# Wider last output-projection products and four unused products around the second layer norm in a one-core decode block

## The chip, the core and the metric

The kernel runs on one core of one Trainium2 chip. The metric is the device time of one execution in microseconds, the median of several runs. A profile of one execution comes with it: when each instruction ran on TensorE (matmuls, PE, and their weight loads, PEld), VectorE (DVE), ScalarE (ACT), GpSimd (POOL) and SyncE (SP), what each waited for, when DMA transfers landed, and which share of its full clock TensorE was granted.

## What is computed

One decode step of a transformer block for four sequences with one token each. The model width is 512. The vector `c` gives six modulation vectors per sequence. The block is attention over the last 1024 cached positions (32 query heads over 8 key/value heads of 128), then a feed-forward layer with 1792 hidden units and ReLU; both have a layer norm in front and a gate behind.

```python
mod = (silu(c) @ w_mod).reshape(4, 6, 1, 512)
sa, ca, ga, sb, cb, gb = (mod[:, i] for i in range(6))
h = layernorm(x) * (1 + ca) + sa
x = x + ga * attention(h, k_cache, v_cache, wq, wo)   # ... @ wo at its end
h = layernorm(x) * (1 + cb) + sb
x = x + gb * (relu(h @ w1) @ w2)
```

Weights and caches are bfloat16; about 32 MB are read from HBM in one execution.

## The kernel before

Every engine's order is the order in which the program is written (a manual schedule). All large loads are issued by SP in one order: `w_mod`, two tiles of the key cache, `wq`, the other keys, the value tiles, `wo` in four parts, `w1`, and `w2` in five chunks that get smaller (512, 512, 384, 256 and 128 KB; they hold the hidden blocks 0 to 3, 4 to 7, 8 to 10, 11 to 12, and 13). Tiles are recycled, so a load is issued when its buffer is free; `w1` and `w2` lie in one buffer, `w12`, that `w_mod` used first.

TensorE's stages: transpose `c` and `x`; transpose keys; modulation products; the first layer norm's sums (a matmul with a matrix of 1/512); query products; scores, key tile by key tile; after the softmax, transposes of the probabilities and products with the values (`oT_ps`, L360); a reordering (`o4_ps`, L410). Then comes the region of the change:

- L424: the first half of the products with `wo`. The attention output, padded to 32 columns per part, is the stationary operand and 512 columns of `wo` stream, in four column groups, into `y4_ps`. DVE and ACT copy the result to `y4` in f32 (L428, L429).
- L432: four f32 products that fold `y4` into the transposed result `y_ps`, with `sel_b` (4 columns) as the moving operand. The profile shows each f32 product as two passes.
- L436: the second half of the products with `wo`. Now blocks of `wo` are stationary, taken with a step of four columns, and the 4 real columns of `o4` stream; 64 products, accumulated into `y_ps`. The first 32 need the third part of `wo`, the others the fourth.
- L441 to L445 on DVE: the gate, the residual sum (`s2`, and `xs2` for later) and its square. L447: one product with the 1/512 matrix gives mean and mean square for the second layer norm (`s_ps`).
- L194 from L451: `closing` turns `xs2` into the layout of the output (`x12_ps`, shown as x_ps). `closing` issues pairs of products with 32 columns of weights each in two column groups.
- L453 to L464 on DVE and ACT: mean, centred value times gain (`ab`), variance, and its inverse root (`rstd2`).
- L484, in `ffn1`: the products with `w1`, 32 for the first eight hidden blocks and 24 for the other six. The moving operand has 8 real columns, repeated four times (32). DVE scales by `rstd2`, adds and applies ReLU (L487 to L490) into `uT32`.
- L194 from L500 and L506: the products with `w2`, again through `closing`, four per hidden block, into `za_ps` (blocks 0 to 3 and 6 to 8) and `z_ps` (the others). 128 columns of `w2` stream in each.
- L502 to L511: ACT copies `za_ps`, DVE multiplies by the gate and adds `x12_ps` (`zc`); when `z_ps` is done, DVE makes `zg` (L509) and `res` (L511), and two DMAs write the output.

`sc_ps`, the PSUM tile of the scores (two banks of 512 columns), is last read by the softmax.

Of the kernel before, what the change touches and what calls it, by code (L numbers as in the profile page):

```python
# [9 lines left out]
ALU = mybir.AluOpType  # L10
AX = mybir.AxisListType
bf16 = mybir.dt.bfloat16
f32 = mybir.dt.float32
# [4 lines left out]
def kernel(  # L18
# [14 lines left out]
    nc = tc.nc  # L33
    P = 128
    B, Sq, D = A_x.shape
# [5 lines left out]
    DT = D // P  # L41
# [3 lines left out]
    CG = 32  # L45
# [17 lines left out]
    const = ctx.enter_context(tc.tile_pool(name="const", bufs=1))  # L63
# [4 lines left out]
    psA = ctx.enter_context(tc.tile_pool(name="psA", bufs=6, space=bass.MemoryType.PSUM))  # L68
# [34 lines left out]
    for h in range(Hkv):  # L103
        vt_ = kvpool.tile([P, NI, Dh], bf16, tag="kv", name=f"v{h}")
        nc.sync.dma_start(
            out=vt_[:].rearrange("p j d -> p (j d)"),
            in_=A_v_cache[:, h, S - W:, :].rearrange("b (p j) d -> p b (j d)", j=NI),
# [5 lines left out]
    NP = Hkv // 2  # L113
    wo_sb = wts.tile([P, NP, NL, D], bf16, tag="big", name="wo_sb")
# [13 lines left out]
    for (m0, e) in W2_CHUNKS:  # L128
        nc.sync.dma_start(out=w2_dst[:, m0 * D:(m0 + e) * D],
                          in_=B_w2[m0 * P:(m0 + e) * P, :].rearrange("(q e) n -> q (e n)", e=e))  # L130
# [3 lines left out]
    ident_bf = const.tile([P, P], bf16, name="ident_bf")  # L134
# [10 lines left out]
    ident_f = const.tile([P, P], f32, name="ident_f")  # L145
# [6 lines left out]
                          in_=ident_f[:].rearrange("p (k c) -> p k c", k=4)[:, :, 0:NX * B:NX])  # L152
# [2 lines left out]
    eps_t = const.tile([P, 1], f32, name="eps_t")  # L155
    nc.gpsimd.memset(eps_t[:], EPS)

    sel_b = const.tile([P, B], f32, name="sel_b")
    nc.vector.tensor_reduce(out=sel_b[:], in_=ident_f[:].rearrange("p (l c) -> p c l", c=CG)[:, 0:B, :], axis=AX.X, op=ALU.add)

    sel_o = const.tile([P, NL, 2, P // NL], bf16, name="sel_o")
    nc.gpsimd.memset(sel_o[:], 0.0)
# [5 lines left out]
    o4 = const.tile([P, NL, 2, 2, CG], bf16, name="o4")  # L168
# [17 lines left out]
    def rows(tile3, j, x):  # L186
        return tile3[:, j, NX - x:NX - x + CG]

    def closing(parts):
        for x in range(NX):  # L190
            for (ps, q, j, src, rhs, start, stop, cols) in parts:
                for g in range(2):
                    q0 = (q + g) * CG
                    nc.tensor.matmul(out=ps[q0:q0 + CG, cols], lhsT=rows(src, j, x), rhs=rhs(2 * x + g),  # L194
                                     start=start and x == 0, stop=stop and x == NX - 1, tile_position=(0, q0))
# [21 lines left out]
    sc_ps = psS.tile([P, W], f32, tag="s", name="sc_ps")  # L217
# [15 lines left out]
    def k_scores(gi, kT):  # L233
        b, par = gi // 2, gi % 2
        for half in range(2):
            for hw in range(NHW):
# [13 lines left out]
                            axis=AX.XY, op=ALU.add)  # L250
# [6 lines left out]
    for t in range(DT):  # L257
        for k in range(4):
            nc.tensor.matmul(out=m4_ps[k * CG:(k + 1) * CG, :], lhsT=rows(siluT32, t, 0), rhs=wmod_sb[:, t, k * D:(k + 1) * D],  # L259
                             start=(t == 0), stop=(t == DT - 1), tile_position=(0, k * CG))  # L260
    for t in range(DT):
        nc.tensor.matmul(out=m5_ps[:], lhsT=rows(siluT32, t, 0), rhs=wmod_sb[:, t, 4 * D:5 * D],  # L262
                         start=(t == 0), stop=(t == DT - 1), tile_position=(0, 0))
# [8 lines left out]
    for t in range(DT):  # L272
        nc.tensor.matmul(out=mT[:, t, 0:4, :].rearrange("p k b -> p (k b)"), lhsT=m4_sb[:, t, :], rhs=ident_m[:],  # L273
                         start=True, stop=True)
# [5 lines left out]
    sa, ca, ga, sb_, cb = [modT[:, k] for k in range(5)]  # L280
# [39 lines left out]
    for t in range(DT):  # L320
        for hq in range(Hq):
            nc.tensor.matmul(out=qT_v[:, hq, :], lhsT=wq_sb[:, t, hq * Dh:(hq + 1) * Dh], rhs=hT[:, t, :],  # L322
                             start=(t == 0 and hq == 0), stop=(t == DT - 1 and hq == Hq - 1))
    for par in range(2):
        dst = qpad_s[:, :, par * NHW * CG:(par + 1) * NHW * CG].rearrange("p b (h c) -> p b h c", h=NHW)
        nc.vector.tensor_copy(  # L326
            out=dst[:, :, :, 16 * par:16 * par + rep],
            in_=qT_ps[:, par].rearrange("p h r b -> p b h r"))
# [35 lines left out]
    for iq in range(NQ):  # L364
        ws = slice(iq * WQ, (iq + 1) * WQ)
        nc.scalar.activation(out=e_sb[:, ws].rearrange("q (u k e) -> q u k e", k=KC, e=2),  # L366
                             in_=sc_ps[:, ws].rearrange("q (u e k) -> q u k e", e=2, k=KC), func=ACT.Exp,
                             bias=nb[:], scale=scale, accum_out=den4[:, iq:iq + 1])
    for iq in range(NQ):
        ws = slice(iq * WQ // 2, (iq + 1) * WQ // 2)  # L370
        nc.vector.tensor_tensor(out=p_w[:, ws, :], in0=e_w[:, ws].unsqueeze(2).to_broadcast([P, WQ // 2, B]),  # L371
                                in1=mi4[:].unsqueeze(1).to_broadcast([P, WQ // 2, B]), op=ALU.bitwise_and)
# [21 lines left out]
    for h in range(VEARLY, Hkv):  # L394
        pv(h, 0, NI, last=(h == Hkv - 1))
        if h == VEARLY:
# [6 lines left out]
                            in0=oT_ps[:].rearrange("p h a b r -> p (h a b r)"), in1=rb[:], op=ALU.mult)  # L403

    o4_ps = psA.tile([P, NL, 2, 2, B, 2], f32, tag="t", name="o4_ps")
    for l in range(NL):
        for a in range(2):
            for rh in range(rep // 2):
                q0 = (2 * a + rh) * CG
                nc.tensor.matmul(out=o4_ps[q0:q0 + CG, l], lhsT=sel_o[:, l].rearrange("p s d -> p (s d)"),  # L410
                                 rhs=oT_sb[:, a::2, :, :, 2 * rh:2 * rh + 2], start=True, stop=True,
# [9 lines left out]
    for g in range(GM):  # L421
        for l in range(NL):
            q0 = l % 4 * CG
            nc.tensor.matmul(out=y4_ps[q0:q0 + CG, :], lhsT=o4[:, l, g % 2, g // 2, :], rhs=wo_sb[:, g, l, :],  # L424
                             start=(g == 0 and l < 4), stop=(g == GM - 1 and l >= 4), tile_position=(0, q0))
    y4 = work.tile([P, DT, P], f32, name="y4")
    y4_src = y4_ps[:].rearrange("p (q t) -> p t q", t=DT)
    nc.vector.tensor_copy(out=y4[:, 0:DT // 2, :], in_=y4_src[:, 0:DT // 2, :])  # L428
    nc.scalar.copy(out=y4[:, DT // 2:DT, :], in_=y4_src[:, DT // 2:DT, :])  # L429
    y_ps = psA.tile([P, DT, B], f32, tag="t", name="y_ps")  # L430
    for t in range(DT):
        nc.tensor.matmul(out=y_ps[:, t, :], lhsT=y4[:, t, :], rhs=sel_b[:], start=(t == 0), stop=False)  # L432
    for g in range(GM, NP):
        for l in range(NL):
            for m in range(DT):
                nc.tensor.matmul(out=y_ps[:, m, :], lhsT=wo_sb[:, g, l, m::DT], rhs=o4[:, l, g % 2, g // 2, 0:B],  # L436
                                 start=False, stop=(g == NP - 1 and l == NL - 1 and m == DT - 1))


    yT = work.tile([P, DT, B], f32, name="yT")  # L440
    nc.vector.tensor_tensor(out=yT[:], in0=y_ps[:], in1=ga, op=ALU.mult)  # L441
    s2 = work.tile([P, 2, DT, B], f32, name="s2")
    nc.vector.tensor_tensor(out=s2[:, 0], in0=yT[:], in1=xcen[:], op=ALU.add)
    nc.vector.tensor_tensor(out=s2[:, 1], in0=s2[:, 0], in1=s2[:, 0], op=ALU.mult)
# [3 lines left out]
                     start=True, stop=True)  # L448
    x12_ps = psA.tile([2 * CG, DH2], f32, tag="t", name="x12_ps")
    for t in range(DT):  # L450
        closing([(x12_ps, 0, t, xs2, lambda j: ident_f[:, j * (P // NH):(j + 1) * (P // NH)], True, True, slice(t, None, DT))])  # L451
    me = work.tile([P, 2, B], f32, name="me")
    nc.vector.tensor_reduce(out=me[:], in_=s2_ps[:].rearrange("p s t b -> p s b t"), axis=AX.X, op=ALU.add)  # L453
    xc2 = work.tile([P, DT, B], f32, name="xc2")
# [90 lines left out]
```

## Time and profile before

| what | value |
|---|---|
| time, median of 4 runs | 85.53 us (85.38, 85.44, 85.61, 85.64) |
| profiled execution, its own time | 85.44 us |
| its span | 83.5 us, 2373 instructions |
| TensorE busy, matmuls / weight loads | 56.4 us / 47.5 us |
| DVE, ACT, POOL busy | 26.4 us, 23.9 us, 5.9 us |
| read from HBM | 31.99 MB, 383 GB/s over the span |
| mean granted clock of TensorE | 0.795 |
| L436, 64 products | 2.4 us busy, mean 173 ns |
| L432, 8 passes | 1.9 us busy, mean 357 ns |

Times of instructions count from the start of the span. The span is shorter than the execution's own time by what lies in front of the first and behind the last instruction. A matmul's duration runs from its start to the end of its result; matmuls overlap, so the distance between two starts, not the duration, says what one more costs. The granted clock is 1.0 or 0.5.

### The profile page before, as it was taken

To read this page: it belongs to the slowest core of one execution; us is meant where nothing else is said; L and a number is where in the kernel's file an instruction comes from. 1 tells how busy PE (TensorE), PEld (TensorE's weight loads), DVE (VectorE), ACT (ScalarE), POOL (GpSimd) and SP (SyncE) were. 2 spreads that over 40 slices of the span, in tenths; PEclk is the share of its full clock that TensorE was granted. 3 is DMA by queue.
4 is the path that set the end of the run, shared out by engine and by line. 5 is a ranking of instruction groups with operands and counts; after the bars stand their busy time and mean duration, and the time that the engine had idled before them with its cause. 6 is when DMAs were issued, how large, how long until landed. Compare 5 with 4: busy or idle time off the path is not lost.

```text
span 83.5 us, 2373 instructions
## 1 busy us (share of the span) xinstructions
PE 56.4 (67%) x1064; PEld 47.5 (57%) x1064; DVE 26.4 (32%) x76; ACT 23.9 (29%) x38; POOL 5.9 (7%) x21
## 2 busy tenths in 40 slices
PE   0001006999972889999999941999817579776950
PEld 0000006995862883997777801999817339666730
DVE  0201300348133100164665476950001320150450
ACT  3201001664302000487788727640100010002010
POOL 5894000000000000000000000000000000000000
PEclk9999999999995555599999999659755555555589
DMA  2899999998999999999999999999999999989600
GB/s 26 321 458 424 408 428 431 522 486 361 408 384 416 424 416 432 408 420 424 424 412 416 432 412 424 412 432 420 412 416 435 408 412 441 440 364 405 258 18 2
DMA packets 4257, 32.14 MB, mean 385 GB/s; under 512 B 528, under 2 KB 664, under 8 KB 1304
## 3 DMA queue, kind: packets, MB, share of 16 engines
q1 hardware_dynamic: 4192, 31.99, 92.3%
q8 instruction: 8, 0.13, 0.6%
q10 hardware_dynamic: 24, 0.01, 0.1%
q0 software_dynamic: 32, 0.00, 0.0%
q14 instruction: 1, 0.01, 0.0%
HBM read 31.99 MB, written 0.00 MB: 383 GB/s over the span
## 4 chain that ended last, share of the span: by engine, by line
DMA 64%; PE 25%; DVE 4%; issue 1%; SPq 1%; ACT 1%; DVEq 0%
DMA w<-in_B_w_dram 26%; DMA v<-in_A_v_cache_dram 24%; DMA k<-in_A_k_cache_dram 14%; PE ktp L225 8%; PE qT_ps L322 4%; PE sc_ps L237 2%; PE za_ps L194 2%; PE mT L273 2%; PE mT L275 2%; PE u_ps L484 1%; PE m_ps L259 1%; PE m_ps L262 1%; PE st_ps_var L289 1%; PE gb_ps L194 1%; SPq L93 0%
## 5 line engine op out<-in xcount | busy, mean ns | idle before, releaser
L225 PE MATMUL ktp<-ident_k,k 128*128 128x128 bf16 x256 | 19.0, 246 | 5.6 <-DMA k<-in_A_k_cache_dram 5.6
L225 PEld LDWEIGHTS <-k 128*128 128x128 bf16 x256 | 17.9, 113 | 8.3 <-DMA k<-in_A_k_cache_dram 5.7
L230 ACT COPY kT<-ktp 128x1024 bf16<-128x1024 bf16 x16 | 15.6, 1015 | 18.0 <-PE ktp L225 17.0
L228 DVE COPY kT<-ktp 128x1024 bf16<-128x1024 bf16 x16 | 11.1, 692 | 17.0 <-PE ktp L225 16.7
L360 PE MATMUL oT_ps<-pT,v 128*128 128x16 bf16 x256 | 7.1, 172 | 1.9 <-issue 1.9
L360 PEld LDWEIGHTS <-v 128*128 128x128 bf16 x256 | 7.0, 100 | 2.0 <-issue 2.0
L237 PE MATMUL sc_ps<-kT,qpad 128*32 128x512 bf16 x64 | 5.6, 445 | 0.4 <-DVE qpad L326 0.4
L377 PE MATMUL pT_ps<-ident_bf,p_rep 128*128 128x128 bf16 x32 | 3.3, 286 | 2.9 <-DVE p_rep L371 2.9
L200 PE MATMUL tp<-ident_bf,cx_sb 8*128 8x8 bf16 x4 | 0.3, 174 | 7.3 <-DMA cx_sb<-in_A_x_dram 7.3
L377 PEld LDWEIGHTS <-p_rep 128*128 128x128 bf16 x32 | 2.9, 133 | 3.4 <-DVE p_rep L371 3.4
L322 PE MATMUL qT_ps<-hT,wq_sb 128*128 128x4 bf16 x128 | 3.6, 166 | 1.4 <-DVE ab L315 1.4
L322 PEld LDWEIGHTS <-wq_sb 128*128 128x128 bf16 x128 | 3.5, 104 | 1.5 <-DMA wq_sb<-in_A_wq_dram 1.5
L200 PEld LDWEIGHTS <-cx_sb 8*128 8x128 bf16 x4 | 0.2, 114 | 7.2 <-DMA cx_sb<-in_A_x_dram 7.2
L429 ACT COPY y<-y_ps 128x256 f32<-128x256 f32 x1 | 0.4, 373 | 9.3 <-DVE y L428 9.3
L402 DVE TENSOR_TENSOR oT_sb<-oT_ps,rb 128x128 bf16<-128x128 f32 x1 | 0.3, 290 | 7.8 <-PE oT_ps L360 7.8
L371 DVE TENSOR_TENSOR p_rep<-e_sb,mi 128x512 int32<-128x512 int32 x4 | 2.5, 685 | 0.7 <-ACT e_sb L366 0.7
L436 PEld LDWEIGHTS <-wo_sb 128*128 128x128 bf16 x64 | 2.5, 120 | 0.3 <-DMA wo_sb<-in_A_wo_dram 0.3
L432 PEld LDWEIGHTS y_ps<-sel_b,y 128*128 128x128 f32 x8 | 1.8, 328 | 1.4 <-DVE y L428 1.4
L436 PE MATMUL y_ps<-o,wo_sb 128*128 128x4 bf16 x64 | 2.4, 173 | 0.3 <-DMA wo_sb<-in_A_wo_dram 0.3
L424 PE MATMUL y_ps<-wo_sb,o 128*32 128x512 bf16 x16 | 1.9, 628 | 0.9 <-DVE o L415 0.9
L237 PEld LDWEIGHTS <-qpad 128*32 128x32 bf16 x64 | 1.3, 103 | 2.2 <-DVE qpad L326 0.7
L194 PEld LDWEIGHTS <-uT 128*32 128x32 bf16 x56 | 2.1, 126 | 0.7 <-DVE uT L490 0.3
(113 smaller groups left out, 56.4 us busy)
## 6 DMA issues: line engine op xcount, KB each, us to landing
k<-in_A_k_cache_dram SPq DMA_DIRECT2D x8, 1024.0 KB, 28.4
v<-in_A_v_cache_dram SPq DMA_DIRECT2D x8, 1024.0 KB, 20.0
wq_sb<-in_A_wq_dram SPq DMA_DIRECT2D x1, 4096.0 KB, 23.1
wo_sb<-in_A_wo_dram SPq DMA_DIRECT2D x4, 1024.0 KB, 20.0
wmod_sb<-in_w_mod_dram SPq DMA_DIRECT2D x1, 2304.0 KB, 9.4
w<-in_B_w_dram SPq DMA_DIRECT2D x1, 1792.0 KB
w<-in_B_w_dram SPq DMA_DIRECT2D x2, 512.0 KB, 19.8
wmod_sb<-in_w_mod_dram SPq DMA_DIRECT2D x1, 768.0 KB, 4.4
```

Source lines behind the costliest of these rows:

```text
L194: nc.tensor.matmul(out=ps[q0:q0 + CG, cols], lhsT=rows(src, j, x), rhs=rhs(2 * x + g), start=start and x == 0, stop=stop and x == NX - 1, ...
L225: nc.tensor.transpose(out=tp[:, ii, :], in_=k_tiles[gi][:, iq * IQ + ii, :], identity=ident_k)
L228: nc.vector.tensor_copy(out=dst, in_=tp[:])
L230: nc.scalar.copy(out=dst, in_=tp[:])
L237: nc.tensor.matmul(out=sc_ps[hw * CG:(hw + 1) * CG, half * HALF:(half + 1) * HALF], lhsT=qpad[:, b, par, hw, :], rhs=kT[:, half * (NI // 2 ...
L322: nc.tensor.matmul(out=qT_v[:, hq, :], lhsT=wq_sb[:, t, hq * Dh:(hq + 1) * Dh], rhs=hT[:, t, :], start=(t == 0 and hq == 0), stop=(t == DT ...
L360: nc.tensor.matmul(out=oT_ps[:, hw, par].rearrange("p b r -> p (b r)"), lhsT=v_tiles[h][:, i, :], rhs=pT[:, i, c0:c0 + B * rep], start=(fi ...
L371: nc.vector.tensor_tensor(out=p_w[:, ws, :], in0=e_w[:, ws].unsqueeze(2).to_broadcast([P, WQ // 2, B]), in1=mi4[:].unsqueeze(1).to_broadca ...
L377: nc.tensor.transpose(out=tp[:, ii, :], in_=p_rep[:, i // 2, :, i % 2], identity=ident_bf[:])
L424: nc.tensor.matmul(out=y4_ps[q0:q0 + CG, :], lhsT=o4[:, l, g % 2, g // 2, :], rhs=wo_sb[:, g, l, :], start=(g == 0 and l < 4), stop=(g == ...
L432: nc.tensor.matmul(out=y_ps[:, t, :], lhsT=y4[:, t, :], rhs=sel_b[:], start=(t == 0), stop=False)
L436: nc.tensor.matmul(out=y_ps[:, m, :], lhsT=wo_sb[:, g, l, m::DT], rhs=o4[:, l, g % 2, g // 2, 0:B], start=False, stop=(g == NP - 1 and l = ...
```

## The change

The products L432 and L436 get 32 moving columns instead of 4: `sel_b` is built with 32 columns, the PSUM tile holds 32 columns per block, and all 32 columns of `o4` stream (the 28 others are zeros, and their results are not read). `y_ps` becomes a view of the first 4 columns. Further, a helper `keep_busy` issues products of the identity with 512 and 256 columns of the last part of `wo` into `sc_ps`, where nothing reads them: one pair after L436, one pair after the `closing` products of `x12_ps`. After the change L432, L436, L447 and L484 are lines 433, 437, 454 and 492; the unused products are line 443.

```diff
-    sel_b = const.tile([P, B], f32, name="sel_b")
-    nc.vector.tensor_reduce(out=sel_b[:], in_=ident_f[:].rearrange("p (l c) -> p c l", c=CG)[:, 0:B, :], axis=AX.X, op=ALU.add)
+    sel_b = const.tile([P, CG], f32, name="sel_b")
+    nc.vector.tensor_reduce(out=sel_b[:], in_=ident_f[:].rearrange("p (l c) -> p c l", c=CG), axis=AX.X, op=ALU.add)
...
-    y_ps = psA.tile([P, DT, B], f32, tag="t", name="y_ps")
+    y32_ps = psA.tile([P, DT, CG], f32, tag="t", name="y_ps")
+    y_ps = y32_ps[:, :, 0:B]
     for t in range(DT):
-        nc.tensor.matmul(out=y_ps[:, t, :], lhsT=y4[:, t, :], rhs=sel_b[:], start=(t == 0), stop=False)
+        nc.tensor.matmul(out=y32_ps[:, t, :], lhsT=y4[:, t, :], rhs=sel_b[:], start=(t == 0), stop=False)
     for g in range(GM, NP):
         for l in range(NL):
             for m in range(DT):
-                nc.tensor.matmul(out=y_ps[:, m, :], lhsT=wo_sb[:, g, l, m::DT], rhs=o4[:, l, g % 2, g // 2, 0:B],
+                nc.tensor.matmul(out=y32_ps[:, m, :], lhsT=wo_sb[:, g, l, m::DT], rhs=o4[:, l, g % 2, g // 2, :],
                                  start=False, stop=(g == NP - 1 and l == NL - 1 and m == DT - 1))
+    def keep_busy(widths):
+        for w in widths:
+            nc.tensor.matmul(out=sc_ps[:, 0:w], lhsT=ident_bf[:], rhs=wo_sb[:, NP - 1, 0, 0:w], start=True, stop=True)
+    keep_busy((512, 256))
...
-    nc.vector.tensor_tensor(out=yT[:], in0=y_ps[:], in1=ga, op=ALU.mult)
+    nc.vector.tensor_tensor(out=yT[:], in0=y_ps, in1=ga, op=ALU.mult)
...
     x12_ps = psA.tile([2 * CG, DH2], f32, tag="t", name="x12_ps")
     for t in range(DT):
         closing([(x12_ps, 0, t, xs2, ...)])
+    keep_busy((512, 256))
```

## The prediction

> **What bounds the kernel now.** I read the page first, then the chain of waits, then the end of the kernel in narrow windows. On the page TensorE is busy 67% of the span, but the DMA row is full until the last slices:
>
> ```profile
> PEclk9999999999995555599999999659755555555589
> DMA  2899999998999999999999999999999999989600
> ...
> q8 instruction: 8, 0.13, 0.6%
> ```
>
> The inputs arrive at 385 GB/s nearly to the end, and TensorE works at half its clock (the 5s) from about slice 28 until just before the end. The chain of waits says what the last stage waits for:
>
> ```profile
> 54.16 21.64 DMA w<-in_B_w_dram
> 75.84 1.25 PE u_ps L484 x32
> ...
> 80.37 0.28 DVE zc L504
> 80.65 0.24 DVE zg L509
> ```
>
> So the first FFN products (L484) start when w1 lands, at 75.80. The change's region must be read against that:
>
> ```profile
> 71.53 1.22 PE L436 MATMUL y_ps<-o,wo_sb 128*128 128x4 bf16 x32 [0.25 <-DMA wo_sb<-in_A_wo_dram]
> ...
> 73.53 0.61 PE L447 MATMUL s_ps<-s,onesD 128*128 128x32 f32 x2 [0.78 <-DVE xs L445]
> ...
> 74.07 1.07 PE L194 MATMUL x_ps<-ident_f,xs 128*32 128x32 f32 x32
> ...
> 75.84 1.88 PE L484 MATMUL u_ps<-ab,w 128*128 128x32 bf16 x56 [0.70 <-DMA w<-in_B_w_dram]
> ```
>
> Every wait of TensorE here ends on a DMA or covers DVE work; after x_ps it idles 0.70 us for w1. The second FFN product waits on DMA again. The DMA issues give issue to landing of the last three chunks of w2 (issued at 61.59, 64.08 and 66.56 in the timeline of SP), so they land near 79.29, 79.88 and 80.26:
>
> ```profile
> w<-in_B_w_dram SPq DMA_DIRECT2D x1, 384.0 KB, 17.7
> w<-in_B_w_dram SPq DMA_DIRECT2D x1, 256.0 KB, 15.8
> w<-in_B_w_dram SPq DMA_DIRECT2D x1, 128.0 KB, 13.7
> ```
>
> The weight loads of the last products, in windows, stop at just these times (columns: us, busy, count, clock, DMA share, GB/s):
>
> ```profile
> 79.75:79.94 0.19, 0.02 (x1) 0.50 0.02 5
> 79.94:80.13 0.19, 0.18 (x8) 0.96 0.00 0
> 80.13:80.27 0.14, 0.08 (x3) 1.00 0.00 0
> 80.27:80.36 0.09, 0.08 (x3) 1.00 0.00 0
> ```
>
> The last four products start between 80.275 and 80.345, the last takes 0.22, and zg starts at 80.60. The other input of that end, zc, is ready at practically the same time. From the last landing at 80.23 on only four products, two DVE operations and the output DMA are left. The note that matters: here the clock opened at 79.96, just in time.
>
> **The clock, by its own windows.** The granted clock changes only on a grid of 3.413 us (59.48, 79.96, 83.37; the grid comes from the profile's clock records). TensorE on that grid:
>
> ```profile
> 56.06:59.48 3.42, 3.42 (x133) 1.00 1.01 422
> 66.30:69.72 3.42, 2.89 (x23) 0.50 1.01 416
> 69.72:73.13 3.41, 2.78 (x67) 0.50 1.03 433
> 73.13:76.54 3.41, 2.31 (x55) 0.50 0.96 386
> 76.54:79.96 3.42, 3.24 (x87) 0.50 0.67 253
> 79.96:80.60 0.64, 0.60 (x12) 1.00 0.00 0
> ```
>
> The busy time does not explain it: 3.42 of 3.42 us closed the clock at 59.48, and 3.24 opened it at 79.96. The columns streamed do. At half clock a column takes 0.83 ns (128-column products start 107 ns apart, 512-column ones 427). Counted so, f32 columns twice since 32 of them take 53 ns, the five full windows hold 30%, 40%, 6%, 45% and 76% of streaming. The clock closed after 30% and opened after 76%; 56%, at 11.69 to 15.10, did not open it. The threshold to open lies between 56% and 76%; the one to stay open is above 30%, and no window tells more.
>
> **The change, part by part.**
>
> *Wider L436.* Sixty-four products get 32 columns instead of 4. They start 33.3 ns apart; the first 32 of L484, also with weights four apart and with 32 columns, start 33.3 ns apart too. The weight load sets this pace, so the cost is the end of the last product only: 192 against 173 ns, +0.02 us. Streaming rises from 3.3 to 26.7 ns in each.
>
> *Wider L432.* Eight f32 passes start 213 ns apart under weight loads of 328. A 32-column f32 pass streams 53 ns, beside the next load: 0, which the row of L447 supports (its two passes, 32 columns wide, start 205 apart). Were it not overlapped: 8 x 0.053 = 0.43, of which the 0.25 wait for wo swallows most and the 0.70 wait for w1 the rest.
>
> *Wider sel_b.* One DVE reduction of 0.50 us at 3.8 us grows; DVE then idles 3.73 us. Nothing. yT reads y_ps with a stride: 16 elements, 0.17 us as the neighbouring rows.
>
> *First pair of unused products.* 512 + 256 columns at 0.83 ns are 0.64 us, from 72.61 to 73.25. With the 0.21 us from streaming to the end of a product (314 less 107 ns) it ends at 73.46, and L447 starts at 73.50 after DVE. Covered. Queued behind it on TensorE: L447, then x_ps; DVE's me waits for L447.
>
> *Second pair.* Streams from 74.95 to 75.59, ends by 75.80; L484 is queued behind it and starts at 75.84. If each weight load in front (about 0.10) stood alone, it ends 0.2 later and L484 slips by up to 0.16. The next cover: the products of the first two w2 chunks end streaming at 79.15 and then wait until 79.32 for the third chunk. So 0 at the end. No gain can come before L484 either, since w1 sets its start.
>
> *The clock.* In this profile's grid the new streaming is 0.85 + 0.85 (L436) + 0.52 (unused) + 0.11 us in the window to 73.13, 68%; and 0.12 + 0.11 + 0.85 + 0.64 + 0.56 in the next, 67%. Both lie between 56% and 76%, so opening at 73.13 or 76.54 is likely, not certain. What is it worth? L484 is paced by weight loads (27 ns at half clock, 25 at full in oT_ps), and the z products wait for landings. So in this execution the gain is 0. But where the grid falls so that the end runs at half clock, it costs: the eight products of the fourth chunk take four steps of 107 from 79.95 to 80.38, the last chunk two more, last start 80.49, +0.31 = 80.80 against 80.56: +0.24 us. The four runs of before are 85.38, 85.44, 85.61, 85.64: two pairs 0.21 apart, as if half of them ended at half clock. That reading is an inference; only one execution was profiled.
>
> **Sum.** The profiled execution: 83.5 span + 1.9 around it = 85.44, 0.09 under the median 85.53. Change to it: 0.00 (covers) + 0.00 (end already at full clock). With the clock open at the end in most runs, the median becomes that of the lower pair, (85.38 + 85.44)/2 = 85.41; with 0.02 for the wider last product's end I say 85.43.
>
> [...]
>
> **Rivals.**
>
> 1. *Opened too early, closed again.* At full clock the window 76.54 to 79.96 streams less: L484 13 ns of each 27, the z products 53 instead of 107 and then stops for landings, together about 45% (0.5 + 0.85 + 0.2 of 3.41). If staying open needs more than that, the clock closes before the end in runs where before it had just opened: every run goes to the upper pair, 85.41 + 0.24 = 85.65. For: 30% was not enough. Against: 45% was never seen at full clock. Chance 0.24.
> 2. *The clock does not open earlier at all.* The threshold is above 68%: 85.53, as before. Chance 0.12.
> 3. *Code loading (slower).* The q8 line is 8 packets with 0.6% of 16 engines' 83.5 us, 1.0 us each. The landings of w1 and w2 fall into two groups some 1.5 us apart, half of the DMA engines late, as one late engine more with each such packet suggests. The change adds 8 TensorE instructions. A ninth packet on a late engine before 79.8 would add up to 1.0 us: 86.4. It decides if the ninth is asked for before the end; the eight came 256 instructions apart on average, the last after 2028 of 2144, so the ninth is due near 2284 and the change reaches 2152. Chance 0.05.
> 4. *Faster than the lower pair:* only if landings move earlier, which nothing in the change does, or if before's middle lies at its upper pair and the change's at 85.3. Chance 0.13.
>
> **How the numbers follow.** Forecast 0.46 (85.43, by itself 85.33 to 85.52), rival 1 0.24, rival 2 0.12, rival 4 0.13, rival 3 0.05. The range 85.30 to 85.72 takes in the forecast, rival 2 and rival 1 with its 0.24 set against either of the lower runs, and leaves out rival 3 and most of 4. 0.3% (0.26 us) is about what a measurement of this kernel can tell from no change: below 85.27 is rival 4, 0.15 with the forecast's edge; above 85.79 is rival 3 and rival 1 with a late L484, 0.13; within, 0.72.
>
> **What would show it.** Right: L437 still 33 ns apart; L484 at 75.8 after w1; the unused products inside the former idle times; the clock row showing 1.0 from near 73 or 76; the last four z products right after the last landing, zg at 80.6. Wrong: L484 waiting for TensorE's own queue, weight loads of z without stops, a ninth q8 packet, or a time below 85.3.

## The result and the profile after

The change made the kernel slower by a quarter of a per cent: 85.61 us median (85.46 to 86.08, 54 runs) against 85.44 us (85.14 to 85.82, 78 runs of the kernel before), ratio 1.0025, 95% interval 1.0019 to 1.0032. The forecast was 85.43 us, 0.10 under the median then known. The measured time lies inside the stated range, but on the other side of the kernel before.

The profiled execution takes 85.58 us, with a span of 83.8. The lines of its page that answer to those of before:

```profile
PEclk9999999999995555599999999659755555555589
DMA  2899999998899999999999999999999999999700
...
q8 instruction: 8, 0.13, 0.6%
```

There is no ninth code packet (8 on q8, as before) and no earlier opening of the clock (80.11 us, against 79.96). The DMA row ends fuller: 9997 where 9896 stood, in slices of 2.1 us. The timeline in the region of the change:

```profile
71.70 1.25 PE L437 MATMUL y_ps<-o,wo_sb 128*128 128x32 bf16 x32 [0.48 <-DMA wo_sb<-in_A_wo_dram]
...
72.79 0.80 PE L443 MATMUL sc_ps<-wo_sb,ident_bf 128*128 128x512 bf16 x2
...
75.26 0.82 PE L443 MATMUL sc_ps<-wo_sb,ident_bf 128*128 128x512 bf16 x2
...
76.01 1.89 PE L492 MATMUL u_ps<-ab,w 128*128 128x32 bf16 x56
```

The products behave as costed: 32 products of 32 columns take 1.25 us instead of 1.22, and the unused ones lie in the former idle times. But L437's second half starts at 71.70 instead of 71.53, and L492 at 76.01 instead of 75.84, each at the landing of its weights. The last three chunks of w2 take 0.1 to 0.2 us longer from issue to landing:

```profile
w<-in_B_w_dram SPq DMA_DIRECT2D x1, 384.0 KB, 17.8
w<-in_B_w_dram SPq DMA_DIRECT2D x1, 256.0 KB, 16.0
w<-in_B_w_dram SPq DMA_DIRECT2D x1, 128.0 KB, 13.8
```

They are also issued 0.09 to 0.12 later, and the last lands at 80.51 instead of 80.23. From that landing to the end of the span it is 3.29 us, against 3.30 before. So between these two executions, whose spans differ by 0.26 us, later landings (0.28 us) are the whole difference, and 0.17 of it is there at 71.7, before either pair of unused products runs. (The executions' own times differ by 0.14 and the medians by 0.17.) The trace's single DMA packets show where it comes from: the 2560 packets of 8192 bytes take 315.3 ns on average instead of 313.7. The first two key tiles, 256 packets, take 309.0 ns in both; the difference begins with the third, at 24.3 us. Each of the 16 DMA engines moves 160 of these packets, and 160 x 1.6 ns is 0.26 us.

What differs at 24 us, long before the wider products? Only `sel_b`. It was built with 128 bytes per partition instead of 16, and every SBUF tile allocated behind it moved by 96 bytes. The program places the buffer of `w_mod`, `w1` and `w2` at byte 25216 of each partition before the change and at 25312 after it; the buffer of `wq` and `wo` and the key and value tiles follow at distances that are multiples of 256, so all share one remainder: 128 above a multiple of 256 before, 224 after.

### The profile page after: what moved, and what is told of

Same layout as the page of the kernel before. It is cut to its first block, busy times and chain, and to the rows that moved or that the text cites. A ratio compares the mean times of both kernels' runs of the same rounds, so it can differ in the third digit from the quotient of the medians.

```text
span 83.8 us, 2381 instructions
## 1 busy us (share of the span) xinstructions
PE 58.0 (69%) x1068; PEld 47.7 (57%) x1068; DVE 26.5 (32%) x76; ACT 23.9 (29%) x38; POOL 5.9 (7%) x21
## 4 chain that ended last, share of the span: by engine, by line
DMA 80%; PE 8%; SPq 4%; DVE 3%; issue 1%; ACT 0%; DVEq 0%
DMA k<-in_A_k_cache_dram 32%; DMA v<-in_A_v_cache_dram 24%; DMA wo_sb<-in_A_wo_dram 24%; SPq L83 3%; PE za_ps L194 2%; PE y_ps L437 2%; PE u_ps L492 1%; PE x_ps L194 1%; PE sc_ps L443 1%; SPq L98 1%; PE s_ps L454 1%; SPq L93 0%; SPq L92 0%; PE z_ps L194 0%; DVE zg L517 0%
## 5 line engine op out<-in xcount | busy, mean ns | idle before, releaser
L437 PE MATMUL y_ps<-o,wo_sb 128*128 128x32 bf16 x64 | 2.5, 194 | 0.5 <-DMA wo_sb<-in_A_wo_dram 0.5
L437 PEld LDWEIGHTS <-wo_sb 128*128 128x128 bf16 x64 | 2.5, 120 | 0.6 <-DMA wo_sb<-in_A_wo_dram 0.6
L433 PEld LDWEIGHTS y_ps<-sel_b,y 128*128 128x128 f32 x8 | 1.8, 327 | 1.4 <-DVE y L428 1.4
```

The costliest lines, as they stand in the source:

```text
L437: nc.tensor.matmul(out=y32_ps[:, m, :], lhsT=wo_sb[:, g, l, m::DT], rhs=o4[:, l, g % 2, g // 2, :], start=False, stop=(g == NP - 1 and l = ...
```

## Experiments

Three theories stood at the outset. A: TensorE's extra streaming makes the last landings later. B: eight more TensorE instructions shift the loading of code. C: the clock opens early, closes, and leaves the end at half clock. After the first four kernels the packet times gave theory D, the addresses. Each ratio is against runs of the kernel before on the same chip, with its 95% interval.

**Wide products alone.** The change without its two calls:

```diff
-    keep_busy((512, 256))
```

> Only the 32-column products (L432, L436), no unused products; the instruction count is that of before. Theory A (TensorE's extra streaming around 70 to 73 us makes the last landings later): part of the +0.17 us, about +0.08 (85.5). Theory B (8 more TensorE instructions shift the loading of code, and landings move with it): 0.00. Theory C (the clock opens early and is closed again before the end, so that the end runs at half clock): the window to 73.1 holds about 52% of streaming, too little to open, so 0.00.

Measured: 85.88 us against 85.59, ratio 1.0044 (1.0025 to 1.0063); packets of 315.3 ns. That is no less than the whole change costs, so the loss comes with the wide products or with what was allocated for them.

**Unused products alone.** Before, plus both `keep_busy` calls:

> Only the four unused products, 4 columns in the others. Theory A: the rest of the +0.17, about +0.1. Theory B: the whole, +0.17. Theory C: the windows to 73.1 and 76.5 hold about 20% and 65%, so the clock opens no earlier in most runs: 0.00 to +0.05.

Measured: 85.49 us, ratio 0.9993 (0.9977 to 1.0010); packets of 313.7 ns. These products stream for about 1.3 us (twice the 0.64 of the prediction) before the last landings, and no cost shows: against theory A.

**Eight instructions more.** Before, with four tiny products early:

```diff
+    for _ in range(4):
+        nc.tensor.matmul(out=sc_ps[:, 0:1], lhsT=ident_bf[:], rhs=ident_bf[:, 0:1], start=True, stop=True)
```

> Before, plus four unused products of one column at 7.5 us, where TensorE waits for the first keys: 8 TensorE instructions more and no streaming that counts. Theory A: 0.00. Theory B: +0.17 as in the whole change. Theory C: 0.00.

Measured: 85.49 us, ratio 1.0004 (0.9985 to 1.0024); packets of 313.6 ns; eight code packets. Theory B falls.

**The kernel before again.**

> The kernel before, unchanged, as one more kernel: the difference that equal programs show, 0.00 within the interval, and the granted clock of each of its runs, to set beside those of the change (0.757 to 0.816). Theory C wants the runs of before and of the change to differ in the clock; theories A and B don't.

Measured: 85.61 us, ratio 1.0009 (0.9996 to 1.0023); packets of 313.6 ns. So the four kernels with the narrow `sel_b` (this, before and the last two) show 313.6 or 313.7 ns, and the two with the wide one 315.3.

**Addresses alone.** Before, with a wider tile of which 4 columns are used:

```diff
-    sel_b = const.tile([P, B], f32, name="sel_b")
+    sel_b32 = const.tile([P, CG], f32, name="sel_b")
+    sel_b = sel_b32[:, 0:B]
```

> Before, with the tile of sel_b allocated with 32 columns as in the change, of which 4 are built and used. No engine does anything else; only, all tiles behind sel_b in SBUF stand 96 bytes further (the weights' buffer at 25312 instead of 25216). Theory D (the loads land at worse addresses, every 8192-byte packet takes 315.3 ns instead of 313.7, and with 160 such packets per DMA engine the last lands 0.26 us later): +0.25 us, ratio 1.003, packets of 315.3 ns. Theory A (TensorE's extra streaming makes the last landings later): 0.00 and 313.7 ns.

Measured: 85.85 us against 85.54, ratio 1.0043 (1.0025 to 1.0062); packets of 315.3 ns. No instruction is added or widened, and the loss is all there, as large as that of the wide products alone. Theory A is out, and the wide products themselves are worth nothing that shows. Every tile behind `sel_b` moved here, and no run moves the load buffers alone; that they are the ones that matter is argued from the packets, which are what got slower.

**64 bytes further.**

> Before, with 64 unused bytes per partition behind sel_b: the weights' buffer at 25280, a multiple of 64, and 192 above a multiple of 256. Theory D in the form that an address off a multiple of 64 costs (before 0, the change 32): 0.00, packets of 313.7 ns. Theory D in the form that the distance above a multiple of 256 costs in proportion (before 128, the change 224, so 0.53 ns per 32 bytes): 314.8 ns, +0.17 us.

Measured: 85.62 us, ratio 1.0003 (0.9983 to 1.0023); packets of 314.3 ns. Near the first form of D, but not quite at it.

**384 bytes further,** a multiple of 512:

> Before, with 384 unused bytes behind sel_b: the weights' buffer at 25600, a multiple of 512. Theory D by multiples of 64: 0.00, 313.7 ns. Theory D by the distance above a multiple of 256 (now 0): 311.6 ns, -0.34 us, ratio 0.996.

Measured: 84.71 us, ratio 0.9904 (0.9881 to 0.9927); packets of 310.2 ns. A multiple of 256 is worth more than the forecast 0.34: it takes 3.5 ns off the mean large packet, where 2.1 was expected.

**The change, moved by 32 bytes more.**

```diff
-    sel_b = const.tile([P, CG], f32, name="sel_b")
+    sel_w = const.tile([P, CG + 8], f32, name="sel_b")
+    sel_b = sel_w[:, 0:CG]
```

> The whole change, with 32 more unused bytes behind sel_b: the weights' buffer at 25344, a multiple of 256. Theory A: as the change, +0.2 us. Theory D by multiples of 64: 0.00, 313.7 ns. Theory D by multiples of 256: 311.6 ns, -0.34 us. Under either form of D the prediction's own question is left by itself: what the wider and the unused products are worth, forecast -0.1 to 0.0 us.

Measured: 84.62 us against 85.54, ratio 0.9894 (0.9873 to 0.9915); packets of 310.2 ns. Thirty-two unused bytes turn the change from a loss of 0.25% into a gain of 1.06%. The windows view shows the mean rate of the loads between 26 and 70 us (columns: us, mean granted clock, DMA share, GB/s). Before, the change, addresses alone, the change moved:

```profile
26.00:70.00 44.00, 0.73 1.01 420
```

```profile
26.00:70.00 44.00, 0.73 1.01 418
```

```profile
26.00:70.00 44.00, 0.73 1.01 418
```

```profile
26.00:70.00 44.00, 0.73 1.01 426
```

The DMA engines are equally full in all four (share 1.01); only the rate differs, and TensorE does nearly the same work in that stretch (the eight wider passes of L433 lie in it). So the packets are slower (313.7, 315.3, 315.3 and 310.2 ns for 8192 bytes), and more waiting does not show. The sums fit: the packets of the load queue (q1) together take each of the 16 engines 77.08 us before and 76.42 in the moved change, 0.65 less, which is most of the 0.76 by which the last landing comes earlier (79.47 instead of 80.23).

**32 above a multiple of 256.**

> Before, with 160 unused bytes behind sel_b: the weights' buffer at 25376, 32 above a multiple of 256. So far the mean 8192-byte packet took 310.2 ns at 0 above, 313.7 at 128, 314.3 at 192 and 315.3 at 224. If the distance counts, 311 ns here and about -0.55 us against before; if being off the multiple costs a step and the distance little, 313 ns and about -0.1 us.

Measured: 85.95 us against 85.55, ratio 1.0053 (1.0028 to 1.0078); packets of 315.4 ns. Neither guess held: this is as bad as 224 above. The five places order themselves roughly by steps (192 lies 0.7 ns above 128, while kernels with one place differ by 0.2 at most):

| above a multiple of 256 | 8192-byte packet, ns | time |
|---|---|---|
| 0 | 310.2 to 310.4 | 84.56 to 84.75 us |
| 128, 192 (multiples of 64) | 313.6 to 314.3 | 85.44 to 85.62 us |
| 32, 224 (not multiples of 64) | 315.3 to 315.4 | 85.61 to 85.95 us |

**What the products are worth at good addresses.** Three kernels with the buffer at 25344: before (called e10 in the expectations), only the unused products, only the wide ones.

> Before, with the loads at exactly the addresses of the moved change (25344): 310.2 ns per packet and -0.8 us, as with 384 bytes. Its last stage runs at half clock in part of the executions, so its times should spread over about 0.2 us or more.

> Only the four unused products, 4 columns in the others, weights' buffer at 25344. If the unused products alone keep the end at full clock: as the moved change, 0.1 us under e10 and with a narrow spread. If the wide products are needed as well: as e10.

> Only the 32-column products, weights' buffer at 25344. If the wide products alone keep the end at full clock: 0.1 us under e10 with a narrow spread. The windows hold too little streaming for that (38% and 67% in the profiled execution of the wide products alone), so as e10.

Measured, against 85.55: before at 25344 84.75 us (84.55 to 84.94), ratio 0.9912 (0.9889 to 0.9936); unused products 84.56 us (84.46 to 84.59), 0.9886 (0.9861 to 0.9912); wide products 84.67 us (84.42 to 84.98), 0.9903 (0.9876 to 0.9930). The intervals overlap, so the gain of 0.1 to 0.2 us is not established by the medians alone. The spreads hint at more: with the unused products (this kernel and the moved change) eleven runs lie within 0.23 us; without them (384 bytes, 25344, wide) eighteen lie within 0.56. But at the old address it does not show: the unused products' twelve runs there lie within 0.56, those of before again within 0.44. The fastest runs with the unused products are no faster than the fastest without them.

The clock explains a part of the spread. Among the runs of before that were measured beside the experiments, 31 of 68 have a mean granted clock under 0.77, about one window of 3.41 us at full clock less than the others; their median is 85.63 us against 85.49. That 0.14 is small beside the 0.88 by which the other 37 runs differ among themselves (85.15 to 86.03). In the kernels with unused products such runs are 3 of 54 (the change), 0 of 12, 0 of 6 and 0 of 5 (the unused products alone, the moved change, the unused products at 25344). What they lose shows in the windows of the end. The profiled execution of before again, then the moved change:

```profile
78.50:79.50 1.00, 1.00 (x32) 0.50 0.47 175
79.50:80.50 1.00, 0.97 (x22) 0.50 0.09 30
80.50:81.50 1.00, 0.39 (x8) 0.50 0.00 0
```

```profile
77.50:78.50 1.00, 0.93 (x32) 0.76 0.59 222
78.50:79.50 1.00, 0.72 (x20) 1.00 0.19 67
79.50:80.50 1.00, 0.30 (x8) 1.00 0.00 0
```

In the first the clock stays at 0.50 to the end, and the span ends 3.52 us after the last landing (80.34); in the second it has opened, and the rest is 3.29 us (from 79.47). All fourteen profiled executions divide in this way: 3.48 to 3.52 us in the five whose last products run at half clock, 3.28 to 3.34 in the nine others.

## Why the prediction was wrong

**The step that failed** is "Wider sel_b": "One DVE reduction of 0.50 us at 3.8 us grows; DVE then idles 3.73 us. Nothing." The instruction was priced, and for it nothing is right (0.50 us in both profiles). The tile was not priced: it grew by 112 bytes, the allocation by 96, and 32 MB of loads landed at worse addresses. That is the term missing from the sum: +0.26 us from the packets, +0.28 in the last landing, +0.43% in the run with the addresses alone. Rival 4 held the same error in words: landings move only if something moves them, "which nothing in the change does". The trace of before could not price it, since all large tiles stand at one remainder there; but the tile's new size was in the diff, and the loads were known to bound the kernel. That 85.61 us still lies in the range is luck: the upper part of the range was there for rival 1, a clock that closes again, and not for slower loads.

**Right:** that the end is set by landings and not by TensorE (a kernel with faster packets, and nothing else changed, is 0.8 us faster); the 33 ns pace of the wider products; the cover of the unused ones (in the kernel with them alone at 25344, w1 lands at 75.01, L492 starts behind the second pair at 75.27, and the end follows the last landing by 3.30 us all the same); the absence of a ninth code packet; and the price of an end at half clock, 0.24 forecast against 3.52 less 3.29. The reading of the first four runs as half open and half closed holds in kind, 31 of 68; the two groups' medians are 0.14 apart, not 0.21, for their ranges overlap.

**Half right:** the forecast gain of 0.10 from the clock. The change at 1.0025 against addresses alone at 1.0043 leaves a gain of 0.15 us, and the moved change against before at a multiple of 256 gives 0.09 to 0.13; these are differences of separate comparisons with overlapping intervals, and the unused products alone at the old address (0.9993) show no gain clear of noise. So a gain of this size is possible, not shown. The cause that was named, an earlier opening, was not what the profiled execution showed. Its windows on the clock's grid (columns as in the prediction):

```profile
69.87:73.28 3.41, 2.92 (x68) 0.50 1.04 436
73.28:76.70 3.42, 3.29 (x58) 0.50 0.95 382
76.70:80.11 3.41, 3.24 (x85) 0.50 0.73 273
```

Counted in columns the first two hold 65% each (forecast 68% and 67%), and neither opened the clock; the third holds 77% and did, at 80.11. For the clock that is rival 2: it does not open earlier. In the profiled execution of the unused products alone at 25344, the window 73.84 to 77.26 held 82% and opened it at 77.26, in time:

```profile
73.84:77.26 3.42, 3.35 (x90) 0.50 0.99 400
77.26:80.67 3.41, 1.89 (x56) 1.00 0.27 101
```

The second pair stands in that window, beside L484's products. But before at 25344, without it, opened at 78.26, also in time for its last landing (79.36), so these two traces decide nothing, and no run has one pair alone, so that this pair earns the gain is argued, not shown. The wide products, which the prediction counted for most of the new streaming, add nothing that shows (84.67 against 84.75 us at 25344, 85.88 against 85.85 at 25312).

**Rival 1**, closing again before the end, shows in none of the profiled executions, and the four runs with the highest mean clocks (0.814 to 0.816) took 84.58, 84.61, 85.48 and 85.58, none slow for its kernel. A mean clock can't tell an early opening that closes again from one late opening, so for the other runs it stays open. The clock closed without an idle window in all fourteen traces, near 57 to 60 us, after a window in which TensorE was busy throughout and streamed 29 to 31% of the time (in the profiled execution of before 3.42 of 3.42 us and 30%, to 59.48). The forecast counts on a clock that, once open, stays open to the end; that was the author's estimate, and no run shows it as a rule. In the execution of before it opened at 56.06 and closed again at 59.48; in the one of the unused products alone at 25344 it opened at 77.26 and was open to the last product.

**The addresses.** The cost does not grow with the distance above a multiple of 256. The mean 8192-byte packet took 310.2 to 310.4 ns at a multiple, 313.6 or 313.7 ns at 128 above and 314.3 at 192, but 315.4 at 32 above and 315.3 at 224. Of the loads, only the place in SBUF that they write was changed, and why the steps lie there is not shown.

## What to carry to other kernels

Where loads bound the kernel, a change to the size of a tile can also change the addresses of all tiles behind it (here 112 bytes more in one tile moved them by 96); compare the placed addresses of both programs before costing anything, and test a suspicious result with an unused tile of the same size. Try starting large load buffers at multiples of 256 bytes: here 128 unused bytes per partition were worth 0.9%, more than the change under study. The five kernels with that padding have the five lowest medians (84.56 to 84.75 us) and are not told apart; the lowest two also have the unused products. Judge a change of some tenths of a per cent only after its layout has been held fixed.

## What the runs showed of the hardware

- The mean 8192-byte load packet took 310.2 to 310.4 ns when its place in the partition was a multiple of 256 bytes, 313.6 to 314.3 ns at other multiples of 64, 315.3 to 315.4 ns 32 off those. Packets of 4096 bytes show the first step alone (159.0 ns against 161.7 to 162.1), those of 3072 more (121.0, then 124.2 to 125.1, then 125.3 to 125.5). Only the places in SBUF were changed, and no other remainder was tried.
- The place is not all of the cause. The 256 packets of 8192 bytes of the first two key tiles took 309.0 to 309.1 ns in every kernel, on or off a multiple of 256; the difference begins with the third tile, at 24.2 to 24.5 us. The code packets (q8) differ too: 0.88 to 0.97 us in the kernels at a multiple of 256, 0.99 to 1.14 in the others. What else it takes, and why there are two steps, is not shown.
- By columns streamed in windows of 3.41 us, the clock opened after 71% and more late in the kernel, and not after 67% or less there. One window at the start of the key transposes, in the unused products' kernel at 25344, did not open it with about 75% by the same count, so the count is only approximate. (The records of the clock begin later; half clock is taken there because the products start 107 ns apart.)
